# A kernel of attention, experts and an MLP: weights prepared in stages, their sums made in place

## The chip, the cores and the metric

The kernel runs on one core of one Trainium2 chip. The metric is the device time of one execution in microseconds. The time given for a kernel is the median of several runs; the profile is one further execution, taken by the hardware profiler, and all rows below come from that one.

## What is computed

Three layers follow one another on 1152 tokens of width 512 (2 batches of 576 positions, 8 heads of 64):

```
attn:  softmax attention on q, k, v averaged over groups of 4 positions, its output repeated 4 times,
       plus softmax attention on a band of |i - j| < 4            -> x (1152 x 512)
moe:   P = softmax-like gates of x @ w_gate, normalised 8 times over rows and columns
       out = sum over 8 experts e of P[:, e] * (relu(x @ w1[e]) @ w2[e])     w1[e] 512 x 1024, w2[e] 1024 x 512
moe2:  h = x @ w_in (512 x 2048);  g = softplus(h);  out = g @ w_out (2048 x 512)
```

All inputs are float32 except `w_in` and `w_out`, which come as float64. The result is float32.

## The kernel before, in words

**Products.** Each operand of a large product is split into a high part, rounded to the matmul's own type, and a low part, the rest; a product is three matmuls (high x high, high x low, low x high) for each of two halves of the contraction. The first product of each layer, x @ w1, is done with seven products of half-size blocks instead of eight (`OPS = 7`). For that, four of the seven weight operands are sums of the four blocks of a weight piece; they are made in `weight_sums`. Each layer's inner dimension is cut in pieces of 2 x 128 columns, four pieces for one of ten "experts" (`NE`: the eight experts, and `w_in`/`w_out` as two more). The tokens are cut in two halves of four and five tiles of 128 (`TILES`).

**Steps.** The list `steps` (line 530) has 80 steps, each one piece for one half of the tokens. A step has seven first products (`first`, six matmuls each, line 601, into PSUM banks `m`) and four or five tiles of second products (`second`, six matmuls each, line 660, into PSUM banks `yps`), so 24 or 30 matmuls at line 660. The main loop (line 792) runs steps 4 to 79; steps 0 to 3 run beside the second half of the attention (`beside`). In the pass of step n, PE does the second products of step n tile by tile, and between the tiles the first products of step n + 2. The results of the first products leave PSUM in `kept` (an ACT copy, line 610) and `combine` (a DVE addition, line 615); `hidden` then makes the high part on ACT (line 558) and the low part on DVE (line 559). `weigh` adds finished second products to the rows of the result on DVE (line 677).

**Weights of an expert.** `fetch_first` and `fetch_second` are called once per piece, when its predecessor of three pieces ago has been used for the last time (`lead`, `used`). `fetch_first` loads the piece to a tile of the tag `raw` (two DMAs on SP's queue, line 124), casts the three plain blocks on ACT (line 132) and subtracts them on DVE (line 133), makes the four sums on POOL (line 111) into two tiles of the tag "sums", casts these on ACT (line 138) and subtracts on POOL (line 139). `fetch_second` loads (line 151), casts on ACT and subtracts on POOL (lines 153, 154). The results go to `w1h`, `w1l`, `w2h`, `w2l`, three buffers each.

**Conversion.** `convert(i)` turns one of 32 pieces of the float64 weights into high and low parts of float32: a DMA to `raw` (lines 169, 174), four bit operations on DVE (178 to 185), ACT's absolute value (186), POOL's addition (188), a DVE multiplication (189). For the 16 pieces of `w_in` it then makes four sums on POOL, casts on ACT (196) and subtracts on POOL (197); all parts are written to `s_in` or `s_out` in DRAM (lines 206, 215 to 217), from where the last two experts load them. It uses one or two tiles of the tag "sums". From step 12 on it is called every one and a half steps, at the end of the pass of a step.

**Buffers.** `raw` has two buffers for all users (pieces of w1, of w2, of the float64 weights), "sums" has two for the sums of a piece of w1 and for the conversion.

**What sets the order.** PE runs the instructions in the order in which the program gives them (`manual_schedule` for PE alone). For the other engines and the DMA queue a planner orders them at compile time, with estimated durations: it takes what is ready in its simulation, and of several the one that stands first in the program; buffers of a tag are given out in program order. On the chip each engine then works its queue in that order, held together by semaphores. All large DMAs are issued on SP's queue.

## Time and profile before

| | us |
|---|---|
| median of 3 runs | 1095.72 |
| lowest and highest | 1094.87, 1096.78 |
| span of the profiled execution | 1094.7 |
| busy in it: PE | 1060.0 |
| DVE | 727.0 |
| ACT | 555.2 |
| POOL | 537.6 |

The matmuls of PE are pipelined, and the profile models their ends, so that consecutive ones overlap and a busy PE may still have gaps between the starts. "Idle" of an engine is the time between the end of one instruction and the start of the next, and the profile names what released the instruction that ended it.

### The profile page before, as it was taken

To read this page: it belongs to the slowest core of one execution; us is meant where nothing else is said; L and a number is where in the kernel's file an instruction comes from. 1 tells how busy PE (TensorE), PEld (TensorE's weight loads), DVE (VectorE), ACT (ScalarE), POOL (GpSimd) and SP (SyncE) were. 2 spreads that over 40 slices of the span, in tenths; PEclk is the share of its full clock that TensorE was granted. 3 is DMA by queue.
4 is the path that set the end of the run, shared out by engine and by line. 5 is a ranking of instruction groups with operands and counts; after the bars stand their busy time and mean duration, and the time that the engine had idled before them with its cause. 6 is when DMAs were issued, how large, how long until landed. Compare 5 with 4: busy or idle time off the path is not lost.

```text
span 1094.7 us, 17873 instructions
## 1 busy us (share of the span) xinstructions
PE 1060.0 (97%) x6385; PEld 938.0 (86%) x6385; DVE 727.0 (66%) x1532; ACT 555.2 (51%) x1443; POOL 537.6 (49%) x569
## 2 busy tenths in 40 slices
PE   6899999999999999999999999999999998999998
PEld 5678888998987889888888988898898897889987
DVE  6889665565666676667657665766663578766765
ACT  4667645343444444434444443444443567676763
POOL 6735235464467676756766455354664212222321
PEclk9579999999999999999999999999999999999999
DMA  8454101111235334434443332223333273244112
GB/s 175 118 115 109 49 27 55 62 58 40 84 100 145 115 110 143 132 105 127 122 134 102 117 112 93 100 93 110 102 116 116 106 278 139 113 175 182 68 39 87
DMA packets 133497, 119.70 MB, mean 109 GB/s; under 512 B 35744, under 2 KB 111776, under 8 KB 133408
## 3 DMA queue, kind: packets, MB, share of 16 engines
q1 hardware_dynamic: 133408, 118.56, 35.0%
q8 instruction: 50, 0.82, 0.3%
q14 instruction: 39, 0.32, 0.1%
HBM read 93.11 MB, written 25.43 MB: 108 GB/s over the span
## 4 chain that ended last, share of the span: by engine, by line
PE 40%; POOL 5%; DMA 5%; DVE 3%; issue 2%; ACT 2%; SPq 0%; POOLq 0%; ACTq 0%; DVEq 0%
PE yps L660 21%; PE m L601 19%; DMA raw<-in_moe_w_out 2%; POOL sums L111 2%; POOL w2l L154 1%; POOL cva L188 1%; POOL cva L197 1%; DMA raw<-in_moe_w 1%; DMA raw<-in_moe_w_in 1%; DVE cva L178 1%; POOL w1l L139 1%; DVE cva L189 0%; DVE cva L179 0%; DVE cva L182 0%; DMA s_out<-cva 0%
## 5 line engine op out<-in xcount | busy, mean ns | idle before, releaser
L601 PE MATMUL m<-xh,w1h 128*128 128x320 f32 (+1 forms) x1120 | 336.6, 301 | 13.1 <-ACT t L610 6.3
L601 PE MATMUL m<-xh,w1l 128*128 128x320 f32 (+1 forms) x1120 | 332.5, 297 | 0.0
L601 PE MATMUL m<-xl,w1h 128*128 128x320 f32 (+1 forms) x1120 | 332.4, 297 | 0.0
L601 PEld LDWEIGHTS m<-xh,w1h 128*128 128x128 f32 x1120 | 212.2, 189 | 38.7 <-ACT t L610 10.8
L601 PEld LDWEIGHTS m<-xl,w1h 128*128 128x128 f32 x1120 | 212.4, 190 | 11.8
L601 PEld LDWEIGHTS m<-xh,w1l 128*128 128x128 f32 x1120 | 212.2, 190 | 0.2 <-issue 0.2
L660 PE MATMUL yps<-w2h,hh 128*128 128x512 f32 x502 | 198.5, 395 | 0.0
L660 PE MATMUL yps<-w2l,hh 128*128 128x512 f32 x502 | 198.4, 395 | 0.0
L660 PE MATMUL yps<-w2h,hl 128*128 128x512 f32 x502 | 195.5, 389 | 0.0
L660 PE MATMUL yps<-w2h,h 128*128 128x512 f32 x436 | 153.3, 393 | 0.0
L615 DVE TENSOR_TENSOR c<-m,t 128x256 f32<-128x256 f32 (+1 forms) x160 | 72.3, 452 | 100.9 <-PE m L601 99.5
L139 POOL TENSOR_TENSOR w1l<-sums,w1h 128x512 fp32r<-128x512 f32 x72 | 95.8, 1345 | 78.2 <-ACT w1h L138 54.4
L571 POOL TENSOR_TENSOR ab<-ab,up 128x320 f32<-128x320 f32 (+1 forms) x64 | 53.9, 843 | 157.2 <-ACT ln L567 109.8
L154 POOL TENSOR_TENSOR w2l<-raw,w2h 128x512 fp32r<-128x512 f32 x72 | 94.9, 1339 | 71.4 <-ACT w2h L153 71.3
L558 ACT ACTIVATE hh<-c 128x256 fp32r<-128x256 f32 (+1 forms) x138 | 60.0, 443 | 125.0 <-DVE c L615 123.3
L559 DVE SCALAR_TENSOR_TENSOR hl<-c,hh 128x256 fp32r<-128x256 f32 (+1 forms) x138 | 91.4, 668 | 35.0 <-ACT hh L558 33.2
L660 PEld LDWEIGHTS yps<-w2h,hl 128*128 128x128 f32 x502 | 94.4, 188 | 21.3
L677 DVE SCALAR_TENSOR_TENSOR acc<-yps,pr,acc 128x512 f32<-128x512 f32 x117 | 86.9, 743 | 29.5 <-PE yps L660 29.4
L660 PEld LDWEIGHTS yps<-w2h,hh 128*128 128x128 f32 x502 | 94.7, 189 | 12.6 <-DVE acc L673 0.2
L660 PEld LDWEIGHTS yps<-w2l,hh 128*128 128x128 f32 x502 | 94.7, 189 | 11.1 <-issue 0.4
L660 PEld LDWEIGHTS yps<-w2h,h 128*128 128x128 f32 x436 | 82.6, 189 | 14.8
L188 POOL TENSOR_TENSOR cva<-cva,raw 128x512 uint32<-128x512 uint32 x32 | 42.7, 1336 | 95.2 <-DVE raw L185 76.6
(134 smaller groups left out, 1700.7 us busy)
## 6 DMA issues: line engine op xcount, KB each, us to landing
raw<-in_moe_w SPq DMA_DIRECT2D x72, 256.0 KB
raw<-in_moe_w SPq DMA_DIRECT2D x36, 512.0 KB
w1h<-s_in SPq DMA_DIRECT2D x10, 896.0 KB
w1l<-s_in SPq DMA_DIRECT2D x10, 896.0 KB
raw<-in_moe_w_in SPq DMA_DIRECT2D x32, 256.0 KB
raw<-in_moe_w_out SPq DMA_DIRECT2D x16, 512.0 KB
w2l<-s_out SPq DMA_DIRECT2D x10, 512.0 KB
w2h<-s_out SPq DMA_DIRECT2D x10, 512.0 KB
```

Source lines behind the costliest of these rows:

```text
L111: nc.gpsimd.tensor_tensor(sums[i], a, b, op=op)
L139: nc.gpsimd.tensor_tensor(lo[:, part], sums, hi[:, part].bitcast(F32), op=ALU.subtract)
L154: nc.gpsimd.tensor_tensor(lo[:, i], raw[:, i], hi[:, i].bitcast(F32), op=ALU.subtract)
L178: nc.vector.tensor_scalar(a, high, 0x07FFFFFF, 3, op0=ALU.bitwise_and, op1=ALU.logical_shift_left)
L188: nc.gpsimd.tensor_tensor(a, a, low, op=ALU.add)
L558: nc.scalar.activation(hh, c, AF.Relu)
L559: nc.vector.scalar_tensor_tensor(out=hl, in0=c, scalar=0.0, in1=hh.bitcast(F32), op0=ALU.max, op1=ALU.subtract)
L571: nc.gpsimd.tensor_tensor(ab, ab, up, op=ALU.subtract)
L601: nc.tensor.matmul(b[:, :h], x[:, i, kk, :], y[s][:, i, kk, :], start=(not more and n == 0), stop=(n == 5), skip_group_check=more,)
L615: nc.vector.tensor_tensor(c, b[:, :h], t, op=ALU.add)
L660: nc.tensor.matmul(y, a[:, f, tok], b[:, f, :], start=(start and m == 0), stop=(stop and m == 5))
L677: nc.vector.scalar_tensor_tensor(out=acc[t], in0=y, scalar=pr[:, t, e : e + 1], in1=acc[t], op0=ALU.mult, op1=ALU.add,)
```

## The change

`fetch_first` and `fetch_second` no longer emit the preparation of a piece of w1 or w2. They allocate the result tiles and put a generator, `make_first` or `make_second`, into the queue `prepare`; `convert` has become a generator as well and goes into the queue `convertings`. In the main loop, after each tile of second products, `advance` runs one piece of the generator at the head of `prepare` (two where more than one generator waits) and one of the head of `convertings`, up to the next `yield`. `make_first` has four stages (DMA; plain blocks; sums; casts and subtractions of the sums), `make_second` two, `convert` six for `w_in` and five for `w_out`. Before the main loop and for its first two steps `finish(prepare)` emits all stages at once; `finish(convertings)` does so when the first piece of the converted weights is fetched.

The four sums of a piece of w1 are written over the four blocks in `raw`, where they are no longer needed, instead of into two tiles of "sums". Their order in the operand tile is another (`PLACE`), for the converted weights too, and `product` reads them by it.

```diff
+    PLACE = (1, 0, 3, 2, 4, 5, 6)
...
+    prepare, convertings = deque(), deque()
+
+    def advance(queue):
+
+        while queue:
+            if next(queue[0], queue) is not queue:
+                return
+            queue.popleft()
+
+    def finish(queue):
+        while queue:
+            for _ in queue.popleft():
+                pass
...
         if e >= E:
+            finish(convertings)
             for i, x in enumerate((hi, lo)):
                 nc.sync.dma_start(x.bitcast(F32), s_in[n - E * NP, i])
             return
+        prepare.append(make_first(e, p, hi, lo))
+
+    def make_first(e, p, hi, lo):
+
         raw = rawp.tile([P, 2, 2, 2, P], F32, tag="raw", name="raw1")
         for fh in range(2):
             nc.sync.dma_start(
...
             )
+        yield
         for part, src in (
             (slice(SUMS, SUMS + 1), raw[:, 0:1, :, 0, :]),
             (slice(SUMS + 1, OPS), raw[:, 1].rearrange("p k f c -> p f k c")),
         ):
             nc.scalar.copy(hi[:, part], src)
             nc.vector.tensor_tensor(lo[:, part], src, hi[:, part].bitcast(F32), op=ALU.subtract)
-        two = [smp.tile([P, 2, 2, P], F32, tag="sums", name="sums") for _ in range(2)]
-        weight_sums([two[i // 2][:, i % 2] for i in range(SUMS)], lambda fh, d: raw[:, d, :, fh, :])
-        for i, sums in enumerate(two):
-            part = slice(2 * i, 2 * i + 2)
+        yield
+        weight_sums([raw[:, d, :, fh, :] for fh, d in ((1, 0), (0, 0), (1, 1), (0, 1))], lambda fh, d: raw[:, d, :, fh, :])
+        yield
+        for d in range(2):
+            part, sums = slice(2 * d, 2 * d + 2), raw[:, d].rearrange("p k f c -> p f k c")
             nc.scalar.copy(hi[:, part], sums)
             nc.gpsimd.tensor_tensor(lo[:, part], sums, hi[:, part].bitcast(F32), op=ALU.subtract)
...
+        prepare.append(make_second(e, p, hi, lo))
+
+    def make_second(e, p, hi, lo):
+
         raw = rawp.tile([P, 2, DM], F32, tag="raw", name="raw2")
         nc.sync.dma_start(raw, w2[e].rearrange("(h a p) d -> p h a d", h=2, p=P)[:, :, p, :])
+        yield
...
-        weight_sums([sums[:, i] for i in range(SUMS)], lambda fh, d: a[:, 2 * d + fh])
+        weight_sums([sums[:, i] for i in PLACE[:SUMS]], lambda fh, d: a[:, 2 * d + fh])
+        yield
...
-                        b[:, :h], x[:, i, kk, :], y[s][:, i, kk, :],
+                        b[:, :h], x[:, place, kk, :], y[s][:, i, kk, :],
...
             fetch_first(f + 3, fetches[f + 3])
+            if n < BESIDE + 2:
+                finish(prepare)
...
                 (fetch_first if i % 2 else fetch_second)((i - 1) // 2, (i - 1) // 2)
+                finish(prepare)
...
+                for _ in range(1 + (len(prepare) > 1)):
+                    advance(prepare)
+                advance(convertings)
...
-                convert(pieces)
+                convertings.append(convert(pieces))
```

The other `yield` lines of `convert` stand behind its DMA, behind the four bit operations, behind POOL's addition and behind the DVE multiplication.

## Rows read from the trace of the kernel before

**Rows 1.** The page, part 1: busy us, share of the span, instructions.

```profile
span 1094.7 us, 17873 instructions
PE 1060.0 (97%) x6385; PEld 938.0 (86%) x6385; DVE 727.0 (66%) x1532; ACT 555.2 (51%) x1443; POOL 537.6 (49%) x569
```

**Rows 2.** Busy time by stretch: PE, PEld, DVE, ACT, POOL, granted clock, DMA.

```profile
270.00:860.00 590.00, 581.02 (x3338) 516.43 (x3337) 381.01 (x650) 255.61 (x566) 345.80 (x344) 1.00 0.36 112
860.00:935.00 75.00, 72.22 (x429) 65.12 (x429) 52.85 (x127) 49.14 (x129) 14.47 (x14) 0.98 0.47 179
```

**Rows 3.** Groups by line, 270 to 860 us: busy, mean ns, idle before, releasers.

```profile
L601 PE MATMUL m<-xh,w1h 128*128 128x320 f32 (+1 forms) x669 | 200.4, 300 | 9.0 <-ACT t L610 3.9 <-DVE c L615 2.0 <-ACT u L610 1.7
L601 PEld LDWEIGHTS m<-xh,w1h 128*128 128x128 f32 x669 | 126.3, 189 | 27.2 <-ACT t L610 7.5 <-DVE c L615 6.2 <-ACT u L610 3.8
```

**Rows 4.** Timeline, 334 to 347 us: start, us, instruction, idle and releaser.

```profile
334.36 1.93 POOL L111 TENSOR_TENSOR sums<-raw 128x256 f32<-128x256 f32 x2 [1.37 <-DMA s_in<-cva]
...
336.31 0.62 ACT L138 CAST w1h<-sums 128x512 fp32r<-128x512 f32 x1 [1.72 <-POOL sums L111]
337.76 2.52 POOL L139 TENSOR_TENSOR w1l<-sums,w1h 128x512 fp32r<-128x512 f32 x2
...
337.83 0.62 ACT L138 CAST w1h<-sums 128x512 fp32r<-128x512 f32 x1 [0.90 <-POOL sums L111]
338.36 0.74 ACT L610 COPY t<-m 128x320 f32<-128x320 f32 x2
...
338.83 0.41 PE L601 MATMUL m<-xh,w1h 128*128 128x320 f32 x1 [0.86 <-ACT t L610]
...
339.05 1.50 DVE L178 TENSOR_SCALAR cva<-raw 128x512 uint32<-128x512 uint32 x1 [3.67 <-POOL w1l L139]
...
346.40 0.42 PE L601 MATMUL m<-xh,w1h 128*128 128x320 f32 x1 [1.01 <-DVE c L615]
```

**Rows 5.** Busy time by stretch, the two disturbed windows (columns as in Rows 2).

```profile
336.00:347.50 11.50, 9.63 (x53) 8.16 (x53) 7.56 (x12) 4.83 (x10) 6.91 (x10) 1.00 0.21 64
482.00:493.50 11.50, 9.77 (x55) 8.30 (x54) 7.64 (x13) 4.65 (x10) 6.98 (x9) 1.00 0.25 78
```

**Rows 6.** Groups by line, 270 to 860 us, steps of a w1 piece.

```profile
L139 POOL TENSOR_TENSOR w1l<-sums,w1h 128x512 fp32r<-128x512 f32 x50 | 66.1, 1334 | 40.8 <-ACT w1h L138 26.4 <-PE yps L660 14.4
...
L111 POOL TENSOR_TENSOR sums<-raw 128x256 f32<-128x256 f32 x50 | 39.6, 812 | 40.9 <-DMA raw<-in_moe_w 31.2 <-DMA s_in<-cva 9.7
...
L133 DVE TENSOR_TENSOR w1l<-raw,w1h 128x256 fp32r<-128x256 f32 (+1 forms) x50 | 31.5, 654 | 6.8 <-ACT w1h L132 5.8
L138 ACT CAST w1h<-sums 128x512 fp32r<-128x512 f32 x50 | 30.7, 617 | 27.9 <-POOL sums L111 27.9
```

**Rows 7.** Line 178: what ended DVE's idle before it (us, times).

```profile
  DMA raw<-in_moe_w_out: 18.3, 8
  POOL w1l L139: 17.4, 13
  DMA raw<-in_moe_w_in: 14.0, 8
```

**Rows 8.** Timeline around 704 us, a conversion of `w_out`.

```profile
702.03 1.30 DVE L178 TENSOR_SCALAR cva<-raw 128x512 uint32<-128x512 uint32 x1 [2.76 <-DMA raw<-in_moe_w_out]
...
704.86 0.68 ACT L186 ACTIVATE raw<-raw 128x512 f32<-128x512 f32 x1 [3.24 <-DVE cva L182]
```

**Rows 9.** Timelines of SP and of PE, 328 to 337 us.

```profile
328.79 0.97 SPq L124 DMA_DIRECT2D raw<-in_moe_w  x2
...
333.48 0.97 SPq L169 DMA_DIRECT2D raw<-in_moe_w_in  x2
...
336.42 0.39 PE L660 MATMUL yps<-w2h,hh 128*128 128x512 f32 x1
```

**Rows 10.** Lines 559 and 615, 270 to 860 us: duration ns min/median/max.

```profile
L559 DVE SCALAR_TENSOR_TENSOR hl<-c,hh x98: 409/602/1583, 269.8 to 854.0; 128x320 fp32r<-128x320 f32 x51, 128x256 fp32r<-128x256 f32 x47
...
L615 DVE TENSOR_TENSOR c<-m,t x94: 406/474/493, 279.4 to 851.2; 128x320 f32<-128x320 f32 x52, 128x256 f32<-128x256 f32 x42
```

More of the change, by code (lines that the diff above doesn't have):

```diff
@@ L1 @@
 from contextlib import ExitStack
+from collections import deque
 from itertools import count
@@ L185, in convert @@
         nc.vector.tensor_scalar(low, low, 28, 1, op0=ALU.logical_shift_right, op1=ALU.bitwise_and)
+        yield
         nc.scalar.activation(high.bitcast(F32), high.bitcast(F32), AF.Abs)
         nc.gpsimd.tensor_tensor(a, a, low, op=ALU.add)
+        yield
         nc.vector.scalar_tensor_tensor(
@@ L197, in parts @@
             engine.tensor_tensor(x.bitcast(F32R), x, hi.bitcast(F32), op=ALU.subtract)
+        yield
         first = raw.rearrange("p d f c -> p (d f c)").bitcast(F32R)
@@ L210, in convert @@
         sums = smp.tile([P, SUMS, P], F32, tag="sums", name="sums")
-        weight_sums([sums[:, i] for i in range(SUMS)], lambda fh, d: a[:, 2 * d + fh])
+        weight_sums([sums[:, i] for i in PLACE[:SUMS]], lambda fh, d: a[:, 2 * d + fh])
+        yield
         parts(sums, first[:, :SUMS], nc.gpsimd)
@@ L597, in product @@
                 b = bank(places[i], f"m{i}")
-            n = 0
+            n, place = 0, PLACE[i]
             for kk in range(2):
@@ L710, in used @@
             fetch_second(f + 3, fetches[f + 3])
+            if n < BESIDE + 2:
+                finish(prepare)
     ready = {}
@@ L747, in attention_moe_mlp @@
                 (fetch_first if i % 2 else fetch_second)((i - 1) // 2, (i - 1) // 2)
+                finish(prepare)
             if j >= 2 and i + 1 < len(units):
```

## The prediction

> **What bounds the kernel now.** I read the page's busy shares first: PE is busy 1060.0 of 1094.7 us [rows 1], so nothing can be won except in the gaps of PE. I then cut the span in stretches. From 270 to 860 us the expert weights are prepared while the float64 weights are converted; there PE has 581.02 busy of 590 us [rows 2], about 9 us of idle. The head up to 165 us (attention) and the change of layer between 860 and 935 us (72.22 of 75 us busy, [rows 2]) also have gaps, but the change hands over nothing new there: the early fetches are still emitted at once, and the second layer's weights are plain loads.
>
> Inside 270 to 860 us the grouped view says who ended the gaps [rows 3]: the first products (L601) waited for the ACT copies of a product (`kept`, L610) and for DVE's `combine` (L615). The three named releasers make 3.9 + 2.0 + 1.7 = 7.6 us of PE idle, and 7.5 + 6.2 + 3.8 = 17.5 us in PE's weight load. A stall costs more than PE's idle, since the modelled end of the matmul before it reaches into the gap, and less than the load's idle, part of which the pipeline hides. I take the middle, 12.6 us, as an estimate of what all these stalls cost; a PE idle microsecond is then worth 12.6 / 7.6 = 1.65 us.
>
> Then the timeline around the worst place shows why ACT and DVE were late [rows 4]. POOL's first sum of a weight block waited 1.37 us for a transfer `s_in<-cva`: the block's sums and the conversion share the two buffers of the tag "sums", and the conversion's had not been written out. The cast L138 behind it kept ACT waiting 1.72 and 0.90 us with the copy L610 in its queue; PE stood 0.86 us. DVE's L178, the next conversion, then waited 3.67 us for that block's last POOL subtraction (L139), for the same buffers, with the combines queued behind; PE stood again at 346.40, 1.01 us. The same pair comes back at 482 us. The two windows leave PE idle 1.87 and 1.73 us [rows 5].
>
> **The change part by part.** Sums in place. Neither instructions nor bytes change: four sums, two casts, two subtractions per block as before [rows 6]. What goes is the sharing of "sums": both windows lose their cause, 3.60 x 1.65 = 5.9 us. DVE's 17.4 us in 13 waits of L178 for L139 [rows 7] can't occur any more either.
>
> In place also adds waits, which this trace does not show. A sum may overwrite a half of `raw` only when L133 has read it, so POOL's L111 now waits for DVE, and what is queued behind it on POOL is the conversion's addition (L188) and its parts (L197), for which DVE's L189 and ACT's L196 wait. And `raw` is given back only after L139. From the first cast on: about 0.6 (cast) + 0.65 (L133) + 4 x 0.8 (L111) + 0.62 (L138) + 2 x 1.33 (L139) [rows 6], about 7.7 us with a little overlap, where L133 alone took it to some 2 us: an estimate of 5 us more for each of the 25 blocks in this stretch (50 casts L138, [rows 6]). The weights themselves are not late: a step lasts about 1060 / 80 = 13 us [rows 1], and a block is used first more than one whole step after its buffer came free. With two `raw` buffers it is the next conversion's transfer that starts later. Sixteen conversions already wait for their own transfer on DVE, 18.3 + 14.0 = 32.3 us or 2.0 us each [rows 7]; the other 13 waited for the buffer, 1.3 us each. The stalls that are left, 12.6 - 5.9 = 6.7 us, belong mostly to those sixteen, as at 702 us, where L178 waited 2.76 us and ACT's L186 behind it 3.24 us [rows 8]: 0.42 us each. If all 13 join them, that is +5.4 us; if their later transfers fall on a DVE that is busy anyway, 0. I see nothing that would make it a gain. I take +2.0, nearer to zero, since a conversion that follows another conversion or a second-layer block gets its buffer as before.
>
> Stages. Each handed-over piece is a generator that advances once per tile of second products. PE keeps its written order; the other engines are ordered by a planner that takes what is ready, the oldest in the program first. The trace shows how far this gate reaches: the transfers L124 at 328.79 and L169 at 333.48 were issued 7.6 and 2.9 us before PE was through step 16 (its successor starts at 336.42; this is the 457th L660 matmul), behind which the code hands both over [rows 9]. So moving them later in the program delays no transfer by itself: SP's queue holds only transfers, they wait there for buffers, and per queue their order stays (block before conversion). What the stages change is who wins when an evacuation and a prepared piece are both ready: L178 of that conversion ran at 339.05 [rows 4], after the handing-over point, ahead of the combines in program order; in stages it comes after those of one more tile. ACT's casts (0.62 us each, [rows 6]) and the conversion's four DVE steps (that L178 took 1.50 us) lose such ties now. That is worth between 0 and the whole rest, 6.7 us. I take -2.5: below the middle, because a queue that waits for a late transfer or a late POOL still blocks what stands behind it, and the stages take no such wait away.
>
> `PLACE` only permutes blocks: no cost. Nothing is added on PE. The sum: -5.9 + 2.0 - 2.5 = -6.4 us, 1094.7 - 6.4 = 1088.3. The median of the runs shown, 1095.72, is 1.0 above the profiled span, so 1089.3.
>
> One rule speaks against the longer POOL chain. DVE instructions with two SBUF inputs stretch here: L559 goes from 409 to 1583 ns, while L615, with one input in PSUM, stays within 406 to 493 [rows 10]. The Trainium skill, "SBUF — State Buffer", section "Who interferes with whom", says that a DVE instruction with two SBUF inputs and a GpSimd instruction that reads SBUF exclude each other for a whole instruction. The trace agrees. By it the six POOL instructions that now follow L133 in a row could each time block the L559 of that moment, 1.58 - 0.41 = 1.2 us of DVE per block, 29 us over 25 blocks; as DVE has 209 us idle there and as many POOL instructions ran beside it before, the sum goes by the row with 0 for it, and by the rule it would be -6.4 us at best.
>
> **The rivals.** *All stalls go.* If ties, not late transfers, cause the rest, the whole 12.6 us goes: 1095.7 - 12.6 = 1083.1. For it: PE waits for evacuations alone, and DVE (381.01 of 590 us) and ACT (255.61) have room for them [rows 2]. Against: 32.3 us of L178's waits are for transfers [rows 7]. Chance 0.17 (below 1087).
>
> *The gain is eaten.* The 13 conversions join those that wait for transfers (+5.4), the stages do nothing: -0.5, 1095.2. For it: the two `raw` buffers are the scarce thing, and blocks hold them 5 us longer. That the planner runs ahead of the handing-over [rows 9], so that the stages don't do what they say, is this case too. Chance 0.20.
>
> *Slower: the chain ACT, DVE, POOL, ACT.* L138 now waits for sums that begin only after L133. Where DVE sits in a wait of L178, L133 is late, POOL is late, and ACT stands before L138 with the copies L610 behind it, as at 336.31 and 337.83 [rows 4]. One such stand costs PE 0.86 x 1.65 = 1.4 us. It decides from 5.9 / 1.4 = 4 of the 25 blocks on; at 8 blocks it is +11.2 - 5.9 = +5.3, 1101.0. For it: L138 already waits 27.9 us in total for the sums [rows 6]. Against: most of these waits cost PE nothing, and part of them came from the shared buffers. Chance 0.20.
>
> **How the numbers follow.** The forecast of 1089.3, with an own range of 1087 to 1093.4, has 0.43. A measurement of this kernel can tell about 0.2%, 2.2 us, from no change: faster is then 0.17 + 0.43 = 0.60, same 0.20, slower 0.20. The range goes from 1083 (all stalls gone) to 1100 (seven or eight blocks stand): it leaves out the upper half of the slower case and what little lies below 1083.
>
> **What would show it.** Right: no wait of L178 for L139 and none of L111 for `s_in<-cva` or `s_out<-cva`; PE's idle in 270 to 860 us down from 9 to about 5 us; L178's waits for its transfers more than 16. The stages' step: fewer L601 gaps ended by L610. The slower rival: L138's wait for L111 above 27.9 us, with L601 gaps at the same times. Wrong altogether would be the forecast if gaps appear before 270 or after 860 us, through a new order of the planner there, or if PE waits for `w1h` or `w2h` themselves.

## The result, and the profile after

The changed kernel takes 1110.18 us (median of 4 runs, 1106.72 to 1118.11), the kernel before, run beside it, 1095.32: a ratio of 1.0145, 95% interval [1.0117, 1.0174]. It is slower by some 15 us, where 1089.3 us was forecast and 1100 was the top of the range. The profiled execution of the changed kernel took 1107.58 us. The page of the kernel after (span, busy us; columns and engines as in [rows 1]):

```profile
span 1105.8 us, 17884 instructions
PE 1062.3 (96%) x6385; PEld 936.2 (85%) x6385; DVE 726.4 (66%) x1532; ACT 554.0 (50%) x1443; POOL 551.9 (50%) x569
```

Each engine has as many instructions as before and PE nearly the same busy time, so the loss is in gaps [rows 1]. Busy time by stretch, after (PE, PEld, DVE, ACT, POOL, granted clock, DMA share, GB/s):

```profile
270.00:860.00 590.00, 570.49 (x3239) 503.73 (x3238) 376.58 (x633) 245.50 (x549) 353.34 (x337) 0.99 0.35 111
860.00:935.00 75.00, 71.27 (x438) 64.06 (x437) 50.27 (x118) 46.74 (x122) 16.82 (x17) 1.00 0.47 176
```

PE has 10.5 us less busy time between 270 and 860 us than before (581.02, [rows 2]). In what follows a *conversion* is one piece of the float64 weights, its *bit operation* the first of DVE's four (L178 before, L206 after), and *the sums* those of a piece of w1. The groups of the first products there (L632, formerly L601: busy, mean ns, idle before, releasers):

```profile
L632 PE MATMUL m<-xh,w1h 128*128 128x320 f32 (+1 forms) x650 | 196.4, 302 | 19.5 <-ACT t L641 8.0 <-ACT u L641 6.8 <-DVE c L646 3.0
...
L632 PEld LDWEIGHTS m<-xh,w1h 128*128 128x128 f32 x650 | 123.0, 189 | 41.1 <-ACT t L641 12.7 <-ACT u L641 11.8 <-DVE c L646 6.9
```

These are the releasers of [rows 3], doubled: PE's idle went from 9.0 to 19.5 us, and most of the growth is ACT's copies `t` and `u`. What ACT, DVE and POOL themselves stood for, by line, 270 to 860 us after (duration ns min/median/max, first and last start; then us, times):

```profile
L206 DVE TENSOR_SCALAR cva<-raw x32: 426/427/1380, 274.7 to 852.9; 128x512 uint32<-128x512 uint32 x32
...
  DMA raw<-in_moe_w_in: 23.8, 15
  DMA raw<-in_moe_w_out: 21.1, 12
...
L160 ACT CAST w1h<-raw x48: 602/621/632, 282.9 to 824.9; 128x512 fp32r<-128x512 f32 x48
...
  POOL raw L126: 51.6, 31
...
L126 POOL TENSOR_TENSOR raw<-raw x96: 727/746/1252, 279.9 to 822.2; 128x256 f32<-128x256 f32 x96
...
  DVE w1l L154: 43.6, 18
...
  DMA raw<-in_moe_w: 2.6, 1
```

L206 is the old L178: its 17.4 us before L139 are gone, but 27 of 32 conversions, not 16, now stand before their own transfer, 44.9 instead of 32.3 us [rows 7]. L126, the old L111, no longer waits for `s_in` or `s_out`; it waits for DVE's subtraction instead, and ACT's cast of the sums (L160, the old L138) waits 51.6 us for it, not 27.9 [rows 6].

A stall from end to end, after (timeline, 504 to 512 us):

```profile
504.24 0.89 SPq L196 DMA_DIRECT2D raw<-in_moe_w_in  x2
...
507.77 0.43 DVE L206 TENSOR_SCALAR cva<-raw 128x512 uint32<-128x512 uint32 x1 [1.69 <-DMA raw<-in_moe_w_in]
...
509.17 0.69 DVE L210 SCALAR_TENSOR_TENSOR cva<-raw,cva 128x512 uint32<-128x512 uint32 x1
...
509.94 0.68 ACT L215 ACTIVATE raw<-raw 128x512 f32<-128x512 f32 x1 [2.95 <-DVE cva L210]
510.52 1.12 ACT L180 CAST w2h<-raw 128x512 fp32r<-128x512 f32 x2
511.55 0.63 ACT L641 COPY t<-m 128x256 f32<-128x256 f32 x2
...
511.96 0.39 PE L632 MATMUL m<-xh,w1h 128*128 128x256 f32 x1 [1.18 <-ACT t L641]
```

The transfer is issued at 504.24. DVE comes to L206 some two microseconds later and stands 1.69 us; L210, the last of those that the conversion's `Abs` needs, is late by that, ACT stands 2.95 us before that `Abs` (L215), two casts follow, and only then come the copies `t` that PE needs.

Not every stall is of this kind. Eight stalls of PE in this stretch are longer than 0.9 us, 13.1 us together. Three of them (at 359.67, 511.96 and 603.71; 4.2 us) stand behind a bit operation that waited 1.77, 1.69 and 0.89 us for its transfer. Three (446.43, 462.00, 562.27; 4.4 us) stand behind ACT's first casts of a weight's piece, which waited 3.89, 0.82 and 1.87 us for theirs; ahead of the last two ACT had also waited for sums of a conversion, 0.71 and 1.96 us. In two (303.28 and 825.04; 4.5 us) DVE's steps of a conversion themselves took long with the combine or ACT's `Abs` behind them: L218 1.75 us at 301.14, L207 and L210 1.67 and 1.10 us from 821.13 on.

From the issue of a conversion's transfer to its first bit operation, the changed kernel leaves 3.1 to 5.2 us in all 32 cases. The kernel before leaves 6.9 to 12.8 us in nine, and after none of these nine does PE have a stall of over 150 ns until the next conversion; after ten of its other 23 PE has one. One of the nine:

```profile
427.00 0.89 SPq L169 DMA_DIRECT2D raw<-in_moe_w_in  x2
```

```profile
434.65 1.50 DVE L178 TENSOR_SCALAR cva<-raw 128x512 uint32<-128x512 uint32 x1 [0.56 <-POOL w1l L139]
```

The wait for the shared buffer that I counted as a cost held L178 back to 7.7 us after the issue, and DVE did six instructions for the first products (L559, L615) and two subtractions (L133) meanwhile. L139 is named as the releaser in seven of the nine. In the six other waits of L178 for L139 it came 3.6 to 5.6 us after the issue, and a stall of PE followed four of them: the shared buffer was a brake in some places and a cost in others.

Where along the run: counting L691's matmuls (24 or 30 a step) gives the start of each step. From step 8 to step 60 the kernel before takes 628.7 us, the changed one 645.1. Steps 0 to 8 take 132.3 us in both; from step 60 to the end it is 237.6 and 238.7. What comes ahead of step 0 (attention) differs from profile to profile, 96.2 us before and 89.7 after, 89.0 to 108.0 over all kernels below. So the change costs 16.4 us in the steps in which weights are converted, and the stretch 8 to 60 is the cleaner measure in what follows.

### The profile page after: what moved, and what is told of

Same layout as the page of the kernel before. It is cut to its first block, busy times and chain, and to the rows that moved or that the text cites. A ratio compares the mean times of both kernels' runs of the same rounds, so it can differ in the third digit from the quotient of the medians.

```text
span 1105.8 us, 17884 instructions
## 1 busy us (share of the span) xinstructions
PE 1062.3 (96%) x6385; PEld 936.2 (85%) x6385; DVE 726.4 (66%) x1532; ACT 554.0 (50%) x1443; POOL 551.9 (50%) x569
## 5 line engine op out<-in xcount | busy, mean ns | idle before, releaser
L632 PE MATMUL m<-xh,w1h 128*128 128x320 f32 (+1 forms) x1120 | 338.2, 302 | 25.2 <-ACT t L641 11.9
L632 PE MATMUL m<-xl,w1h 128*128 128x320 f32 (+1 forms) x1120 | 332.4, 297 | 0.1
L632 PE MATMUL m<-xh,w1l 128*128 128x320 f32 (+1 forms) x1120 | 332.5, 297 | 0.0
L632 PEld LDWEIGHTS m<-xh,w1h 128*128 128x128 f32 x1120 | 212.2, 190 | 54.8 <-ACT t L641 17.5
L632 PEld LDWEIGHTS m<-xl,w1h 128*128 128x128 f32 x1120 | 212.6, 190 | 12.1 <-DVE ex L413 0.4
L632 PEld LDWEIGHTS m<-xh,w1l 128*128 128x128 f32 x1120 | 212.5, 190 | 0.3 <-issue 0.2
L691 PE MATMUL yps<-w2h,hh 128*128 128x512 f32 x502 | 199.3, 397 | 0.3 <-DVE acc L704 0.3
L691 PE MATMUL yps<-w2l,hh 128*128 128x512 f32 x502 | 199.1, 397 | 0.0
L691 PE MATMUL yps<-w2h,hl 128*128 128x512 f32 x502 | 196.8, 392 | 0.0
L126 POOL TENSOR_TENSOR raw<-raw 128x256 f32<-128x256 f32 x144 | 127.4, 885 | 97.0 <-DVE w1l L154 79.6
L691 PE MATMUL yps<-w2h,h 128*128 128x512 f32 x436 | 152.8, 392 | 0.0
L646 DVE TENSOR_TENSOR c<-m,t 128x256 f32<-128x256 f32 (+1 forms) x160 | 72.0, 451 | 99.6 <-PE m L632 94.7
L590 DVE SCALAR_TENSOR_TENSOR hl<-c,hh 128x256 fp32r<-128x256 f32 (+1 forms) x138 | 88.1, 647 | 48.2 <-ACT hh L589 46.8
L589 ACT ACTIVATE hh<-c 128x256 fp32r<-128x256 f32 (+1 forms) x138 | 60.1, 443 | 109.7 <-DVE c L646 108.0
L691 PEld LDWEIGHTS yps<-w2h,hl 128*128 128x128 f32 x502 | 94.9, 189 | 21.8 <-issue 0.2
L691 PEld LDWEIGHTS yps<-w2h,hh 128*128 128x128 f32 x502 | 95.3, 190 | 12.9 <-DVE acc L704 0.5
L161 POOL TENSOR_TENSOR w1l<-raw,w1h 128x512 fp32r<-128x512 f32 x72 | 98.3, 1367 | 15.4 <-ACT w1h L160 15.4
L708 DVE SCALAR_TENSOR_TENSOR acc<-yps,pr,acc 128x512 f32<-128x512 f32 x117 | 86.9, 743 | 28.4 <-PE yps L691 27.9
L691 PEld LDWEIGHTS yps<-w2l,hh 128*128 128x128 f32 x502 | 95.3, 190 | 10.9
```

Of the source, the lines that this page charges most:

```text
L126: nc.gpsimd.tensor_tensor(sums[i], a, b, op=op)
L161: nc.gpsimd.tensor_tensor(lo[:, part], sums, hi[:, part].bitcast(F32), op=ALU.subtract)
L589: nc.scalar.activation(hh, c, AF.Relu)
L590: nc.vector.scalar_tensor_tensor(out=hl, in0=c, scalar=0.0, in1=hh.bitcast(F32), op0=ALU.max, op1=ALU.subtract)
L632: nc.tensor.matmul(b[:, :h], x[:, place, kk, :], y[s][:, i, kk, :], start=(not more and n == 0), stop=(n == 5), skip_group_check=more,)
L646: nc.vector.tensor_tensor(c, b[:, :h], t, op=ALU.add)
```

## The experiments

In all kernels: "bits" is the first bit operation on DVE waiting for its transfer, "sums" the cast of the sums on ACT waiting for POOL, "casts" ACT's first casts of a weight's piece waiting for their transfer (us, times; 270 to 860 us); "idle" is PE's idle ahead of the first products (9.0 in [rows 3]); "8-60" the us from step 8 to step 60. Each ratio is to the kernel before run beside that kernel, 1095.3 us in the first two rows and 1096.4 to 1097.2 us in the others. The waits and stretches are those of one profiled execution each. The expectations give TensorE's stalls by another count (32 us after, 15.7 us before); the profile's idle is the number to compare here.

| kernel | us | ratio to before | bits | sums | casts | idle | 8-60 |
|---|---|---|---|---|---|---|---|
| before | 1095.3 | | 32.3, 16 | 27.9, 20 | 2.2, 1 | 9.0 | 628.7 |
| after | 1110.2 | 1.0145 [1.0117, 1.0174] | 44.9, 27 | 51.6, 31 | 17.9, 14 | 19.5 | 645.1 |
| inplace_only | 1113.1 | 1.0131 [1.0089, 1.0173] | 45.8, 26 | 49.6, 31 | 20.0, 15 | 21.2 | 648.3 |
| tmp9 | 1096.5 | 1.0000 [0.9974, 1.0025] | 37.6, 17 | 28.4, 20 | 2.3, 1 | 10.3 | 631.0 |
| own9 | 1119.8 | 1.0194 [1.0155, 1.0232] | 47.0, 25 | 5.3, 7 | 2.1, 1 | 22.5 | 652.5 |
| own9_staged | 1121.1 | 1.0207 [1.0169, 1.0245] | 44.1, 28 | 4.7, 7 | 4.9, 2 | 24.6 | 656.7 |
| after_gate3 | 1115.0 | 1.0166 [1.0142, 1.0190] | 15.5, 9 | 47.4, 31 | 65.8, 32 | 27.7 | 652.0 |
| before_gate3 | 1114.5 | 1.0168 [1.0147, 1.0190] | 7.6, 5 | 41.8, 32 | 28.0, 17 | 24.4 | 646.5 |
| own9_gate3 | 1108.4 | 1.0103 [1.0085, 1.0122] | 3.3, 2 | 28.0, 23 | 28.1, 20 | 17.8 | 640.0 |
| pool_cast | 1099.9 | 1.0042 [1.0013, 1.0071] | 26.8, 20 | on POOL | 35.7, 30 | 12.9 | 634.4 |
| raw3_t9 | 1113.0 | 1.0148 [1.0117, 1.0179] | 51.8, 27 | 54.1, 32 | 0 | 20.7 | 644.7 |
| raw3_pool | 1096.7 | 0.9999 [0.9980, 1.0017] | 28.0, 20 | on POOL | 2.2, 1 | 8.9 | 626.1 |
| raw3_gates_pool | 1093.6 | 0.9965 [0.9948, 0.9982] | 1.9, 1 | on POOL | 5.8, 5 | 8.1 | 625.8 |
| before_pool_cast | 1117.3 | 1.0177 [1.0132, 1.0221] | 14.1, 7 | on POOL | 33.3, 20 | 9.3 | 633.9 |
| raw3_gates | 1101.2 | 1.0037 [1.0022, 1.0053] | 2.5, 1 | 39.6, 30 | 0 | 11.4 | 630.2 |
| raw3_late_cast | 1110.9 | 1.0130 [1.0105, 1.0154] | 47.8, 19 | 0.5, 1 | 5.1, 2 | 18.8 | 643.3 |
| raw3_allgates | 1104.2 | 1.0062 [1.0041, 1.0083] | 5.5, 4 | 0 | 15.2, 9 | 12.0 | 633.2 |
| before_raw3_pool | 1109.0 | 1.0112 [1.0080, 1.0144] | 3.7, 5 | on POOL | 0 | 6.3 | 624.7 |
| best1 | 1095.5 | 0.9983 [0.9969, 0.9997] | 2.1, 1 | on POOL | 5.4, 5 | 8.0 | 625.4 |
| best2 | 1094.0 | 0.9978 [0.9964, 0.9993] | 30.8, 20 | on POOL | 2.1, 1 | 8.4 | 625.6 |

### Which part of the change costs the time

inplace_only keeps the sums in place and emits everything at once:

```diff
-        prepare.append(make_first(e, p, hi, lo))
+        for _ in make_first(e, p, hi, lo):
+            pass
...
-                convertings.append(convert(pieces))
+                for _ in convert(pieces):
+                    pass
```

> The changed kernel with its sums in place and PLACE, but every generator emptied where it is made, so that preparation and conversion are emitted at once as before. Theory chain (in place, the sums of a piece start only after DVE's subtractions, ACT's cast of the sums waits behind them with the copies of products in its queue, and raw is held until POOL's last subtraction, so the next transfers start late): this part alone is slow, 1105 to 1115 us, with ACT's cast of the sums waiting about 50 us for POOL and the conversion's first DVE step waiting about 45 us for its transfer. Theory stages (handing the pieces over late is what costs): about 1090 us, faster than before, since the shared buffers are gone. Theory reshuffle (any edit gives the planner another order, and stalls come and go without a pattern): anything from 1090 to 1112, with waits that do not go with the time.

own9 is the kernel before with the sums of a weight's piece in buffers of their own, and tmp9 its control (nine working buffers instead of eleven make the room):

```diff
-    tmpp = ctx.enter_context(tc.tile_pool(name="tmpp", bufs=11))
+    tmpp = ctx.enter_context(tc.tile_pool(name="tmpp", bufs=9))
...
-        two = [smp.tile([P, 2, 2, P], F32, tag="sums", name="sums") for _ in range(2)]
+        two = [smp.tile([P, 2, 2, P], F32, tag="own", name="own") for _ in range(2)]
```

> The kernel before with 9 instead of 11 buffers for the temporary results of the products. It is the control for the next two, which need the room. All theories: 1095 us if the two buffers are spare; up to some us more if not. Theory reshuffle: it may move by several us in either direction.

> The control with the two tiles of sums of a w1 piece under a tag of their own, so that they no longer share buffers with the conversion, but are not made in place and nothing is handed over in stages. It measures the first term of the prediction by itself: 5.9 us faster than the control by the prediction. Theory chain: 4 to 7 us faster than the control. Theory reshuffle: no fixed sign.

own9_staged adds the change's stages to own9.

> The same with preparation and conversion handed over in stages, sums in tiles of their own. It measures the stages without the in-place chain. Prediction: 2.5 us faster than with own buffers alone. Theory chain: equal or up to 4 us faster than with own buffers alone, so about 1087. Theory stages: 10 to 18 us slower than with own buffers alone, about 1100 to 1108.

Measured: 1113.1, 1096.5, 1119.8 and 1121.1 us. Taking the sharing away is enough to lose the time, with the sums in place (+1.3%) and, more so, without (+1.9%); the control loses nothing. The stages change nothing that can be told: after against inplace_only, own9_staged against own9, whose intervals overlap. And in own9 ACT hardly stands before sums, 5.3 us, so the chain is not needed for the loss. Its bit operation (L178) and first products, own9, 270 to 860 us:

```profile
L178 DVE TENSOR_SCALAR cva<-raw x31: 411/428/1346, 281.1 to 854.5; 128x512 uint32<-128x512 uint32 x31
...
  DMA raw<-in_moe_w_out: 24.7, 12
  DMA raw<-in_moe_w_in: 22.3, 13
```

```profile
L601 PE MATMUL m<-xh,w1h 128*128 128x320 f32 (+1 forms) x648 | 196.8, 304 | 22.5 <-DVE c L615 9.4 <-DVE h L559 8.2 <-ACT t L610 2.3
```

Here it is DVE's instructions that PE waits for, and DVE stands before transfers 47.0 us. Late transfers aren't all of it in own9. Its four stalls behind `h` (L559, 8.2 us) each follow two subtractions L133 that took 2.8 to 3.3 us together; L133's median is 1092 ns here and 679 ns in tmp9, and DVE is busy 736.6 us instead of 723.3. At 303.00, for one, POOL's subtraction L139 ran from 298.60 to 301.34 beside them. No run takes this second loss away by itself.

### Giving the transfer more time, or taking the cast off ACT

The gate puts the conversion's operations three tiles of second products behind the transfer, not one, and queues the bit operation behind the last combine given out before it:

```diff
-        yield
+        for _ in range(3):
+            yield
...
-        nc.vector.tensor_scalar(a, high, 0x07FFFFFF, 3, op0=ALU.bitwise_and, op1=ALU.logical_shift_left)
+        with tc.issue_after(getattr(behind[0], "ins", behind[0])):
+            nc.vector.tensor_scalar(a, high, 0x07FFFFFF, 3, op0=ALU.bitwise_and, op1=ALU.logical_shift_left)
...
-            nc.vector.tensor_tensor(c, b[:, :h], t, op=ALU.add)
+            behind[0] = nc.vector.tensor_tensor(c, b[:, :h], t, op=ALU.add)
```

> The changed kernel, but the conversion waits three tiles of second products instead of one between its transfer and its first bit operation, and that bit operation (L178 of the kernel before, L206 of the changed one) is queued on VectorE behind the last combine given out before it. So VectorE can't reach it before the transfer has had some 7 us, where the changed kernel gave it 3 to 6. Theory 'late landing' (VectorE stands before a bit operation whose transfer has not landed, with combines queued behind it, and this is where TensorE's stalls come from): the waits of the bit operations for transfers fall from 44.9 us to under 10 us between 262 and 870 us, TensorE's stalls of over 150 ns from 32 us to under 20 us, and the time to 1092 to 1098 us. Theory 'chain' (ScalarE stands before the cast of sums that GpSimd has not made, 52.1 us, 32 times): these waits are untouched by the edit, so 1105 to 1112 us.

> The kernel before, with that edit alone: the transfers of a conversion are given out where they were, its operations three tiles of second products later, its first bit operation behind the last combine. In the kernel before 16 of 32 bit operations waited 32.3 us in all for transfers, while 13 waited for a shared buffer instead. 'Late landing': the 16 waits go and with them part of the 15.7 us of TensorE's stalls: 1088 to 1095 us. 'Chain': no change, 1094 to 1097 us. If the later hold of the raw buffer costs the next piece's transfer its start: 1098 to 1105 us.

> The kernel before with the sums of a weight's piece in buffers of their own (1119.8 us without this edit, the slowest of the unstaged ones) and the edit of the conversion: bit operations three tiles later and behind a combine. Here ScalarE never waits for GpSimd's sums. 'Late landing': what was lost when the shared buffers went comes back: 1092 to 1102 us. If the loss of this kernel has another source (pieces of weights prepared earlier, for example): 1114 to 1122 us.

pool_cast is the changed kernel with one line replaced:

```diff
-            nc.scalar.copy(hi[:, part], sums)
+            nc.gpsimd.tensor_copy(hi[:, part], sums)
```

> The changed kernel with the cast of the sums of a weight's piece (L160) on GpSimd, behind the sums themselves, instead of on ScalarE: ScalarE no longer stands before sums that are not there yet. 'Chain': the 52.1 us of ScalarE's waits go and with them the copies' delays: 1095 to 1101 us. 'Late landing': the bit operations still wait some 45 us for transfers: 1105 to 1113 us, the upper end if GpSimd's own casts lengthen its turn.

Measured: 1115.0, 1114.5, 1108.4 and 1099.9 us. own9 got back 11.4 of its 23 us, short of the 1092 to 1102 expected. The changed kernel gained nothing (the intervals overlap) and the kernel before lost 1.7%, both outside all that was expected. The gate did its work on DVE, and the wait moved to ACT, after_gate3, 270 to 860 us:

```profile
L153 ACT CAST w1h<-raw x48: 400/512/625, 278.6 to 828.0; 128x256 fp32r<-128x256 f32 x24, 128x512 fp32r<-128x512 f32 x24
...
  DMA raw<-in_moe_w: 38.1, 20
```

The bit operations' waits fell from 44.9 to 15.5 us, but ACT's first casts of a weight's piece now stand 65.8 us before transfers (17.9 without the gate). With two `raw` buffers a conversion that keeps one longer would make the next piece's transfer late; that these waits are gone with a third buffer, below, speaks for it. So late landing could not be judged with two buffers. pool_cast gave the 10 us that the chain theory asked for; its times lie between 1093.2 and 1108.9 us, and its profile, in the table, is of the slowest, so that its row says little about the median.

### A third buffer

raw3_t9 is the changed kernel with

```diff
-    rawp = ctx.enter_context(tc.tile_pool(name="rawp", bufs=2))
+    rawp = ctx.enter_context(tc.tile_pool(name="rawp", bufs=3))
...
-    tmpp = ctx.enter_context(tc.tile_pool(name="tmpp", bufs=11))
+    tmpp = ctx.enter_context(tc.tile_pool(name="tmpp", bufs=9))
```

> The changed kernel with three buffers for the raw pieces instead of two, and nine working buffers instead of eleven to make room (nine cost the kernel before nothing: 1.0 [0.997, 1.003]). A transfer that the raw buffers held back starts earlier. Theory 'hold' (the second term of the prediction: in place, a raw piece is held until the last subtraction has read it, so the next transfer starts late): the waits of VectorE's first bit operation (44.9 us) and of ScalarE's first casts (17.9 us) for transfers shrink by more than half, and the time goes to 1098 to 1104 us. Theory 'early plan' (these waits come from where the planner puts the reading instruction, right behind the landing that it reckons with, however early the transfer starts): the waits stay within a third of what they are, 1105 to 1112 us.

raw3_pool adds pool_cast's line; raw3_gates_pool adds the gate too, and a like one for ACT (three tiles, and the first casts L153 and L180 inside `tc.issue_after` of the last copy L641).

> The same third buffer, and the cast of the sums on GpSimd as in pool_cast (1099.9 us). 'Hold': both cures add, 1088 to 1095 us. 'Early plan': the third buffer adds nothing, 1097 to 1103 us.

> Third buffer, cast of the sums on GpSimd, and every first reader of a transfer three tiles of second products behind it: the first bit operation queued behind the last combine on VectorE, the first casts of a weight's piece behind the last copy of partial sums on ScalarE. No engine that TensorE waits for should then stand before a transfer or before GpSimd's sums. If standing before late inputs is the whole loss of the changed kernel (chain and late landing together): waits for transfers under 10 us on both engines, TensorE's stalls of over 150 ns at or under those of the kernel before (15.7 us), time 1085 to 1095 us. If something else takes the time: over 1100 us, with these waits gone.

before_pool_cast is pool_cast's line in the kernel before.

> The kernel before with the cast of the sums (L138) on GpSimd: in it ScalarE stood 27.9 us, 20 times, before these sums. 'Chain': about half of what the same edit gave the changed kernel (10 us for 52.1 us of waits), 1089 to 1094 us. If the cast on GpSimd only shifts its work: 1094 to 1100 us.

Measured: 1113.0, 1096.7, 1093.6 and 1117.3 us. The third buffer alone gives nothing: ACT's casts no longer wait for transfers, and DVE does so as much as before, raw3_t9:

```profile
L206 DVE TENSOR_SCALAR cva<-raw x32: 418/428/1419, 270.4 to 848.5; 128x512 uint32<-128x512 uint32 x32
...
  DMA raw<-in_moe_w_in: 32.6, 15
  DMA raw<-in_moe_w_out: 19.2, 12
```

```profile
L632 PE MATMUL m<-xh,w1h 128*128 128x320 f32 (+1 forms) x648 | 196.4, 303 | 20.7 <-ACT t L641 9.7 <-DVE c L646 8.2 <-ACT u L641 1.8
```

An earlier transfer has its reader put just as close behind it (3.2 to 5.0 us from issue to bit operation): "early plan" for DVE, though the time is 1 us above the range named for it. For ACT's first casts "hold" was right, 17.9 us to none, but this was worth nothing in time. That the planner reckons with an earlier landing than the chip's is inferred from this; what it reckons with is in no trace. raw3_pool lies just below the range of "early plan". With gates and the cast on POOL, raw3_gates_pool, all the loss is gone, and 0.35% of the time of the kernel before; this run met its expectation (waits 1.9 and 5.8 us, idle 8.1 us).

before_pool_cast lies 17 us above the higher of its two ranges. Its conversion steps cost 5.2 us more than before (8-60), and 12.6 us are lost in steps 0 to 8 (144.9 instead of 132.3 us), where the same line also runs.

### Which cure does it

> raw3_gates_pool without the cast on GpSimd: third buffer, the first readers of transfers three tiles later and behind a combine or a copy, but the cast of the sums again on ScalarE, planned where the sums should be ready. Between 262 and 870 us VectorE should no longer stand before transfers, ScalarE still before GpSimd's sums (52 us in the changed kernel). 'Chain is most of it': 1105 to 1112 us, hardly better than with the third buffer alone (1113.0). 'Late landing is most of it': 1094 to 1100 us.

> The changed kernel with the third buffer (1113.0 us), and the cast of the sums, still on ScalarE, three tiles of second products later and queued behind the last copy of partial sums given out before it. No work changes its engine: only the place of the cast in ScalarE's queue. 'Chain' (the place is the cause): ScalarE's waits for GpSimd's sums fall from 54.6 us to under 15 us and the time to that of raw3_pool, 1094 to 1101 us. If raw3_pool (1096.7 us) owed its gain to the work taken off ScalarE: 1106 to 1113 us.

> Both: first readers of transfers and the cast of the sums all three tiles later and behind a copy or combine, third buffer, every operation on the engine that the changed kernel has it on. Standing before late inputs as the whole loss: 1087 to 1095 us, like raw3_gates_pool (1093.6 us). If the cast on GpSimd gave more than its place in the queue: 1098 to 1108 us.

> The kernel before with the third buffer, nine working buffers and the cast of the sums on GpSimd: raw3_pool (1096.7 us) without the sums in place and without the stages. If these two bring something once the late inputs are away: slower than raw3_pool, 1100 to 1118 us (the cast on GpSimd alone gave 1117.3 us here). If they bring nothing: 1093 to 1099 us.

raw3_gates is raw3_gates_pool without the line of pool_cast. raw3_late_cast has only this on top of raw3_t9:

```diff
-        yield
+        for _ in range(3):
+            yield
         for d in range(2):
...
-            nc.scalar.copy(hi[:, part], sums)
+            with after_copy():
+                nc.scalar.copy(hi[:, part], sums)
```

where `after_copy()` is `tc.issue_after` of the last copy L641. Measured: 1101.2, 1110.9, 1104.2 and 1109.0 us. raw3_gates lies 1 us above the range of "late landing" and 4 below that of "chain"; the other three lie in the range of their last-named or slower case. raw3_gates, 270 to 860 us, windows, bit operation (L220), cast of the sums (L168) and first products (L646):

```profile
270.00:860.00 590.00, 578.57 (x3325) 515.32 (x3324) 408.90 (x646) 251.10 (x559) 357.59 (x338) 1.00 0.37 112
```

```profile
L220 DVE TENSOR_SCALAR cva<-raw x32: 410/622/1414, 299.5 to 859.2; 128x512 uint32<-128x512 uint32 x32
...
  DMA raw<-in_moe_w_out: 2.5, 1
...
L168 ACT CAST w1h<-raw x48: 602/621/624, 298.3 to 829.6; 128x512 fp32r<-128x512 f32 x48
...
  POOL raw L132: 39.6, 30
```

```profile
L646 PE MATMUL m<-xh,w1h 128*128 128x320 f32 (+1 forms) x666 | 198.8, 299 | 11.4 <-ACT t L655 8.6 <-DVE c L660 1.8 <-ACT u L655 0.9
```

raw3_late_cast, the same lines (L168 the cast, L214 the bit operation):

```profile
L168 ACT CAST w1h<-raw x48: 616/624/640, 301.8 to 829.5; 128x512 fp32r<-128x512 f32 x48
...
  POOL raw L132: 0.5, 1
...
L214 DVE TENSOR_SCALAR cva<-raw x32: 417/428/1514, 274.6 to 846.8; 128x512 uint32<-128x512 uint32 x32
...
  DMA raw<-in_moe_w_out: 25.2, 11
  DMA raw<-in_moe_w_in: 22.6, 8
```

This decides between the two theories of waiting. Move ACT's cast of the sums, so that its waits for them are gone (54.1 to 0.5 us): 2.0 us are gained, within the intervals, and 1.3 us in steps 8 to 60. Take DVE's waits for transfers away, 51.8 to 2.5 us, and leave ACT before the sums 39.6 us: 11.8 us are gained, although steps 0 to 8 became 7.5 us longer (139.6 instead of 132.1). In steps 8 to 60 it is 14.5 of the 16.0 us by which raw3_t9 is above the kernel before. raw3_allgates, with both, is no better than the gates alone, but ACT's first casts stand 15.2 us in it. So the chain stood there in the trace, and where it was taken away hardly anything was gained.

One theory of the first expectation (that of inplace_only) is left, that any other order costs something like this ("reshuffle"). The times alone don't exclude it: before_gate3 and before_pool_cast, two edits of the kernel before that leave its shared buffers as they are, cost 1.7 and 1.8%. Against it stands that the waits do go with the time. With the cast on ACT, the kernels whose bits and casts come to more than 45 us together take 643.3 us or more from step 8 to 60, and the two with less than 21 us take 630.2 and 633.2; the four in between, 31 to 40 us, lie between 628.7 and 646.5, and there the waits do not tell the time.

The gain of the cast on POOL (16.2 us from raw3_t9 to raw3_pool) is therefore not one of place alone. It takes 48 casts of 0.62 us, 30 us, off ACT, which the copies wait for; it also came with bit operations that waited half as long (51.8 to 28.0 us). The two aren't separated. It and the gates aren't additive (11.8 and 16.2 apart, 19.4 together), and best2 carries 30.8 us of waits for transfers, the kernel before 32.3, at a PE idle of only 8.4 and 9.0 us. I read this so, that a late bit operation hurts PE when ACT has work queued behind it; no run shows it by itself, and the kernel before, with the cast on ACT, fits it only in part. before_raw3_pool has the shortest conversion steps of all, 624.7 us, without sums in place and without stages: neither is worth anything there. The gates in the kernel before with a third buffer, the other cure without the change, were not run. Its 1109.0 us, which by its expectation would say that the two bring something, come from its start (step 0 at 108.0 us) and steps 0 to 8 (136.1 us).

### A version that beats both?

best1 and best2 are raw3_gates_pool and raw3_pool with the cast on POOL, and the gates on ACT's casts, only from the main loop on:

```diff
-            nc.gpsimd.tensor_copy(hi[:, part], sums)
+            (nc.gpsimd.tensor_copy if started[0] else nc.scalar.copy)(hi[:, part], sums)
```

> raw3_gates_pool (1093.6 us) with its three edits in force only once the weights are prepared in stages: before that (attention and the first eight steps) the cast of the sums is on ScalarE and no cast is tied to a copy, as in the changed kernel. There step 8 of the products began at 222.0 us in the changed kernel, at 227.1 us in raw3_gates_pool. If these edits lengthened the head: some 5 us less, 1086 to 1091 us. If the head's length is the planner's accident: 1091 to 1097 us.

> raw3_pool (1096.7 us; step 8 at 227.7 us) in the same manner: the cast on GpSimd only once weights are prepared in stages, third buffer throughout, no instruction tied to another. If the cast on GpSimd lengthened the head: 1089 to 1094 us; otherwise 1094 to 1099 us. Against best1 it tells what the later first readers bring when the cast is on GpSimd: by the stretch from step 8 to 60 (626.2 us in raw3_pool, 625.8 us in raw3_gates_pool) nothing.

Measured: 1095.5 and 1094.0 us. Steps 0 to 8 are back at 132.8 and 132.7 us (138.1 and 135.1 with the edits in the head), as meant, and the times didn't follow as far as hoped: step 0 began at 96.5 and 97.2 us in the profiles, not at 89.0 and 92.6. Why the attention part's length differs from kernel to kernel stays open. best1, best2 and raw3_gates_pool lie 0.2 to 0.35% below the kernel before, all with intervals below 1, and below the changed kernel by 1.3 to 1.5%.

## Why the prediction was wrong

**What bounds the kernel** held: PE waits for ACT's copies and DVE's combines, and for almost nothing else, 7.6 of 9.0 us before [rows 3] and 17.8 of 19.5 after. So did the price of PE's idle: 10.5 us more of it go with 16.4 us in the conversion steps, 1.56 us for each, where the estimate was 1.65.

**Sums in place, -5.9 us: the sign was wrong.** This is the step that failed. Two signs announced came: no wait of L178 for L139, none of L111 for `s_in<-cva` or `s_out<-cva`. But PE's idle went to 19.5 us and not to 5. The step "both windows lose their cause" took a wait for a gain in full. With the shared buffers gone, the bit operation came earlier behind its transfer and stood before that instead. The runs: own9 +1.9%, inplace_only +1.3%, control 0.

**Raw held longer, 0 to +5.4, taken +2.0: right event, wrong cause, too small a size.** I wrote that the 13 conversions might join the 16 that wait for their transfer; 27 wait now, so 11 joined. But it is not that `raw` is held longer (raw3_t9: a third buffer changes neither DVE's waits nor the time). And I took a price per wait, 0.42 us, from the kernel before, where these waits cost little. It is no constant: 32.3 us of waits go with 9.0 us of PE idle, 51.8 us with 20.7. This term, bounded at 5.4, is the one that would have had to be some 15.

**Stages, -2.5 us: nothing.** after and inplace_only can't be told apart, nor can own9_staged and own9. That the planner runs ahead of the point where a piece is handed over [rows 9], which I had put under *the gain is eaten*, agrees with it: all 32 bit operations come within 5.2 us of the issue of their transfer, and within 5.8 us without the stages (inplace_only).

**The slower rival** had the sign of the result and the sign announced for it (ACT before sums: 51.6 against 27.9 us), and the wrong mechanism: raw3_late_cast took that wait away and gained 2.0 us. Its price of 1.4 us per stand falls with it: the 32 stands of raw3_t9 gave 2.0 us. The sign that I named for this rival would have been seen whether it was the cause or not. What came about is nearest to *the gain is eaten* (more conversions wait for their transfers), at some three times the +5.4 us that I had as its upper bound, and with no gain beside it to be eaten.

**The rule that speaks against the longer POOL chain** was put at 0, and in the sum that was right: DVE is busy 726.4 us after and 727.0 before. In single places it was not. At the two stalls behind long DVE instructions (303.28 and 825.04, 4.5 us) POOL worked on a piece of w1, L126 and L161, and L207, L210 and L218 each ended 0.55 us after the POOL instruction that had begun before them.

**Head and tail**, which I left out of the sum: in the two profiles attention is 6.5 us shorter, steps 0 to 8 take 132.3 us in both, and the end is 1.2 us longer. With the 16.4 us of the conversion steps this makes the 11.1 us between the two profiled spans.

## What to carry to other kernels

A wait that a profile shows can be what keeps a worse wait from occurring. Before pricing its removal as a gain, look at what the released instruction reads, and whether that is there by the earlier time. Where the order on an engine is planned ahead, give the first reader of a transfer slack on purpose, by tying it behind a combine or a copy, and give the transfer a buffer more: in the changed kernel neither gained anything without the other. And a long wait on an engine is evidence for a cause only when a run without it is faster: taking 54 us of ACT's waits away gained 2.

## What the hardware showed that I hadn't expected

After a stall of PE the granted clock can fall, and the stall then costs more than its own length. The windows around the stall at 303 us, after (PE busy, granted clock, DMA share, GB/s):

```profile
301.20:303.20 2.00, 0.07 (x1) 1.00 0.00 0
303.20:306.70 3.50, 3.42 (x11) 0.53 0.68 206
306.80:309.30 2.50, 2.50 (x18) 1.00 0.93 263
```

```profile
300.42 0.40 PE L691 MATMUL yps<-w2h,hh 128*128 128x512 f32 x1
300.65 0.39 PE L691 MATMUL yps<-w2l,hh 128*128 128x512 f32 x1
...
303.28 0.51 PE L632 MATMUL m<-xh,w1h 128*128 128x256 f32 x1 [2.01 <-DVE c L646]
...
304.65 0.63 PE L691 MATMUL yps<-w2h,hh 128*128 128x512 f32 x1
305.07 0.63 PE L691 MATMUL yps<-w2l,hh 128*128 128x512 f32 x1
```

The second products follow one another at 0.23 us before the stall and at 0.42 us after it, until 306.8: at a mean granted clock of 0.53, so nearly all of that stretch at the lower of the two levels (1.2 GHz). Of the four stalls of PE of over 2 us after 270 us, two were followed by such a stretch, this one and the one of 2.45 us at 825.04; those of 2.15 us at 462.00 and 2.42 us at 925.44 were not. From 3.5 us at 0.53 and 0.58 of the clock I estimate some 1.5 us in each of the two, about 3 of the 16.4 us lost.

With the gates on, DVE's instructions became longer and PE gained all the same: in raw3_gates the bit operation's median is 622 ns, 428 in raw3_t9, and DVE is busy 408.90 instead of 377.93 us between 270 and 860 us. What lies beside a bit operation decides its length. In raw3_gates the 11 with no POOL instruction beside them took 410 to 420 ns, and 2 beside which POOL started or ended within 0.06 us of their start took 427 and 428. The other 19 began while a POOL instruction ran, took 527 to 1414 ns, and each ended 0.28 to 0.29 us after that instruction had ended. One of them (timeline, raw3_gates):

```profile
510.79 1.48 POOL L169 TENSOR_TENSOR w1l<-raw,w1h 128x512 fp32r<-128x512 f32 x1
...
511.38 1.18 DVE L220 TENSOR_SCALAR cva<-raw 128x512 uint32<-128x512 uint32 x1
```

The same holds in the kernel before: 13 free ones at 426 to 429 ns, and 19 that ended 0.28 to 0.29 us after the POOL instruction beside them, ten of these at about 1.5 us. The Trainium skill, "SBUF — State Buffer", section "Who interferes with whom", says that a `tensor_scalar` may enter a mode in which DVE and GpSimd exclude each other for a whole instruction. The trace agrees: the bit operation looks as if it did its work only once POOL's instruction was through.
